# Retention and two expert layers on one core: q, k and v laid out by pairs of heads, states without zero blocks

## The chip, the cores and the metric

The kernel runs on one core of one Trainium2 chip. The metric is the time of one execution on the device, in microseconds (us). All data are float32. The engines are TensorE (PE in the rows; PEld are its weight loads), VectorE (DVE), ScalarE (ACT), GpSimd (POOL) and SyncE (SP), which here only issues copies.

## The reference, cut to what matters

```python
def _attn_ref(q, k, v):                      # each 4 x 8 x 576 x 64
    scale = 1.0 / np.sqrt(D_)
    scores = scale * np.matmul(q, k.transpose(0, 1, 3, 2))
    gamma = 1.0 - 2.0 ** (-5.0 - np.arange(H, dtype=np.float32))
    rel = pos[:, None] - pos[None, :]
    Dmat = np.where(rel >= 0, gamma[:, None, None] ** rel[None, :, :], 0.0)
    return np.matmul(scores * Dmat[None, :, :, :], v).astype(np.float32)
...
def reference(**kwargs):
    attn_out = _attn_ref(**attn_kwargs)
    x = np.ascontiguousarray(attn_out.transpose(0, 2, 1, 3)).reshape(B * S, H * D)
    x = _moe_ref(x=x, **moe_kwargs)
    return _moe2_ref(x=x, **moe2_kwargs)
```

The first step is a causal attention without softmax, whose weights decay by a power of `gamma` of the head. Its 2304 rows of 512 go through two expert layers (8 experts, 512 to 1024 to 512; one expert per row). The change is in the first step alone.

## The kernel before, in words

**Units.** `attention` (line 118) works in 20 units, five per batch. A main unit is a pair of heads over the first 512 positions, in four chunks of 128; four of them cover the eight heads. The fifth, the tail unit (`tail(u)`), has the last 64 positions of all eight heads. `gamma ** (i - j)` is split: q is multiplied by a power of its position (`qp`), v by the inverse power of its own (`vh`). Then a chunk needs no decay inside, and all chunks before it are summed in one state of 64x64 a head, the sum of k-transposed times vh.

**The steps of a unit.**
- `load` (133): SP copies q, k and v from their natural layout, k and v of each head apart: five copies of a main unit, six of a tail. A head's row of 64 values is a piece of 256 bytes (q: four rows, 1 KB).
- `prep` (170): `qp` and `vh`, on GpSimd from unit 2 on.
- `transposes` (191): TensorE turns k (part 0) and `qp` (part 1) chunk by chunk into PSUM, against the identity; ScalarE copies them to `kT` and `qT`.
- `scores` (207): eight matmuls, for each chunk and head kT by qT over 64 rows, the two heads in two row halves of the array and in two PSUM banks; VectorE multiplies with the mask `tri` into `P`.
- `state` (221): eight matmuls of 64 columns, k by vh, the two heads in two column halves; VectorE adds them up chunk by chunk and head by head into a 128x128 tile with a head's 64x64 state in each diagonal block. The other two blocks are zero from a memset at the start (lines 1513 to 1514).
- `inter` (240): the state before a chunk times that chunk's qT, three matmuls with 128x128 weights into the bank `O`; for a tail unit four, with the states after 512 positions, `st4`.
- `pv` (254): eight matmuls, vh by P, onto the same bank `O`, the heads in two column halves; ScalarE copies `O` to `xT`, the transposed output.

**Order.** `round_(u)` (284) interleaves the units: it prepares and transposes unit u+1, does `inter` of u-1, `scores` of u, `pv` of u-1 and `state` of u+1, and issues the copies of u+5. `slot()` puts a piece of background work between the steps: for a finished batch the router's logits (`logits4`, `token_logits`), the router itself (`Router.add`) and `row`, which transposes a tile of 128 rows back (`xps`) so that GpSimd can write it to its expert's list (`put`, line 486). When the rows of the first two batches are written, `gather` copies the rows of the first expert (`xb`), and the expert weights follow on SP. In `manual_schedule` the engines named in it (TensorE and GpSimd from round 1 on) run in the order of the code; a scheduler orders the others. The MoE behind it starts with `h` of its first place (line 851).

**PSUM.** Eight banks: two for transposes, two for scores, one for `state`, one for `O`, two for the background.

Of the kernel before, what the change touches and what calls it, by code (L numbers as in the profile page):

```python
# [53 lines left out]
TAB0, TAB1 = 72, 336  # L54
# [6 lines left out]
def host_tables():  # L61
# [3 lines left out]
    qtab = np.zeros((128, 4, 4, 2))  # L65
    for h in range(H):
        for t in range(5):
            vtab[:, h // 2, t, h % 2] = gam[h] ** (-(128.0 * t + p))
        for r in range(4):
            qtab[:, h // 2, r, h % 2] = gam[h] ** (4.0 * p + r) / 8.0  # L70
    tl = lambda sg: np.stack([[[gam[4 * j + 2 * a + h] ** (sg * (512.0 + t)) for h in range(2)] for a in range(2)] for j in range(2) for t in range(64)])
# [3 lines left out]
        "qtab": qtab.reshape(128, 32),  # L75
        "tri": p[:, None] <= p[None, :],
        "tri2": (p[:, None] <= p[None, :]) & (p[:, None] // 64 == p[None, :] // 64),
        "vtl": tl(-1).reshape(128, 4),
        "qtl": tl(1).reshape(128, 4) / 8.0,
# [17 lines left out]
    return {"tab": np.ascontiguousarray(tab)}, off  # L97
# [20 lines left out]
def attention(g, hooks):  # L118
# [6 lines left out]
    q, k, v = g.ia["q"], g.ia["k"], g.ia["v"]  # L125
# [7 lines left out]
    def load(u):  # L133
        s = st[u] = K()
        b, p = s.b, s.p = u // 5, u % 5
        if tail(u):
            s.raw = g.ld.tile([128, 3, 2, 2, DH], F32, tag="t", name=f"t{b}", bufs=2)
            for i, x in enumerate((k, q, v)):
                for j in range(2):
                    nc.sync.dma_start(out=s.raw[64 * j:64 * j + 64, i].rearrange("p a h d -> p (a h) d"),  # L140
                                      in_=x[b, 4 * j:4 * j + 4, 512:576].rearrange("h p d -> p h d"))
            return
        hs = slice(2 * p, 2 * p + 2)
        s.q = g.ld.tile([128, 2, 4, DH], F32, tag="q", name=f"q{u}")
        s.k = g.ld.tile([128, 4, 2, DH], F32, tag="k", name=f"k{u}")
        s.v = g.ld.tile([128, 4, 2, DH], F32, tag="v", name=f"v{u}")
        dq = lambda: nc.sync.dma_start(out=s.q, in_=q[b, hs, 0:512].rearrange("h (p r) d -> p h r d", r=4))

        def pair(x, d):
            for hh in range(2):  # L150
                nc.sync.dma_start(out=d[:, :, hh], in_=x[b, 2 * p + hh, 0:512].rearrange("(t p) d -> p t d", p=128))  # L151

        part = lambda c0, c1: nc.sync.dma_start(out=g.tab[:, c0:c1], in_=g.ia["tab"][:, c0:c1])
        if u:
            dq()
            pair(k, s.k)
        else:
            pair(k, s.k)
            part(0, TAB0)
            dq()  # L160
        pair(v, s.v)
        if u == 0:
            part(TAB0, TAB1)
        elif u == 3:
            part(TAB1, g.tab.shape[1])
            g.small_loads()
        elif u == 10:
            g.clear(1)

    def prep(u):  # L170

        s = st[u]
        s.vh = g.wk.tile([128, 4, 2, DH], F32, tag="vh", name=f"vh{u}", bufs=3)
        if tail(u):
            bc = [128, 2, 2, DH]
            s.qp = g.wk.tile([128, 4, 2, DH], F32, tag="qp", name=f"qp{u}")
            nc.gpsimd.tensor_mul(s.qp[:, 0:2], s.raw[:, 1], g.qtl[:, :, :, None].to_broadcast(bc))
            nc.gpsimd.tensor_mul(s.vh[:, 0:2], s.raw[:, 2], g.vtl[:, :, :, None].to_broadcast(bc))
            return
        s.qp = g.wk.tile([128, 4, 2, DH], F32, tag="qp", name=f"qp{u}")  # L180
        (nc.vector if u <= 1 else nc.gpsimd).tensor_mul(s.qp, s.q.rearrange("p h r d -> p r h d"),
                                                        g.qtab[:, s.p, :, :, None].to_broadcast([128, 4, 2, DH]))
        (nc.gpsimd if u else nc.vector).tensor_mul(s.vh, s.v, g.vtab[:, s.p, 0:4, :, None].to_broadcast([128, 4, 2, DH]))  # L183

    def flat(x):
        return x.rearrange("p h d -> p (h d)")
# [3 lines left out]

    def transposes(u, part):
        s = st[u]
# [1369 lines left out]
```

## Time and profile before

| | |
|---|---|
| median of three runs (lowest, highest) | 530.03 us (528.41, 531.34) |
| the profiled execution, its span | 528.95 us, 527.2 us |
| TensorE busy in the span | 507.8 us |
| VectorE, ScalarE, GpSimd busy | 300.3, 226.7, 142.4 us |
| `scores` of unit 0, of unit 4, of unit 19 start | 8.28, 29.32, 101.52 us |
| first expert matmul starts | 105.86 us |

The span goes from the first to the last instruction. A row of the timeline merges like instructions that follow each other; it gives start and length, the engine, the line of the kernel and what the instruction writes and reads, and in brackets the idle time before it with what ended it. TensorE runs one float32 matmul as two instructions (a transpose as one), so a count x8 in its timeline is four matmuls of the code. Ends of matmuls are modelled, so the cost of a step is best read from its start to the start of the next one.

### The profile page before, as it was taken

What the parts mean: (1) busy time and instruction counts of PE and PEld (TensorE: products, weight loads), DVE (VectorE), ACT (ScalarE), POOL (GpSimd) and SP (SyncE); (2) the same over time, 40 slices, a digit from 0 to 9 for tenths busy, and PEclk for the clock granted to TensorE, in tenths of its full rate; (3) what the DMA queues carried; (4) which work ended last, traced back from release to release, by engine and by line L of the source; (5) the groups of instructions that cost most, each with busy time, mean ns of one, the idle gap of its engine ahead of it and who ended that gap; (6) DMA issues with size and microseconds to landing.
All of it is one profiled execution on the core that took longest, in us unless ns stands there. A gap on an engine that the chain in (4) does not pass through costs nothing.

```text
span 527.2 us, 12238 instructions
## 1 busy us (share of the span) xinstructions
PE 507.8 (96%) x4427; PEld 478.0 (91%) x4427; DVE 300.3 (57%) x914; ACT 226.7 (43%) x440; POOL 142.4 (27%) x216
## 2 busy tenths in 40 slices
PE   7989999999999999999999999999999999999993
PEld 6779898799999999999999999999899889999992
DVE  6756668644537675857585866553656765522012
ACT  2344454333445554846464746432444434321120
POOL 3443748441204030230305070604210311110111
PEclk9999999999999999999999999999999999999997
DMA  8789996864989548475766755506769999988800
GB/s 198 165 206 196 255 218 167 268 252 152 291 224 286 164 150 222 142 207 187 203 203 191 212 176 179 158 16 187 244 199 326 320 282 256 312 280 281 278 35 33
DMA packets 133483, 109.64 MB, mean 208 GB/s; under 512 B 57477, under 2 KB 111109, under 8 KB 133413
## 3 DMA queue, kind: packets, MB, share of 16 engines
q1 hardware_dynamic: 127077, 94.69, 64.3%
q0 software_dynamic: 6336, 14.07, 7.2%
q8 instruction: 37, 0.61, 0.5%
q14 instruction: 33, 0.27, 0.2%
HBM read 93.44 MB, written 20.17 MB: 216 GB/s over the span
## 4 chain that ended last, share of the span: by engine, by line
PE 86%; DVE 4%; SPq 3%; DMA 3%; issue 1%; ACT 1%; POOL 1%; DVEq 0%; POOLq 0%; ACTq 0%
PE h L851 13%; PE y L927 9%; PE h L863 7%; PE h L862 7%; PE h L861 7%; PE y L931 6%; PE y L932 6%; PE y L930 6%; PE S L216 3%; PE yr L972 3%; PE O L258 3%; PE y L924 2%; SPq L151 2%; PE xps L656 2%; PE O L252 2%
## 5 line engine op out<-in xcount | busy, mean ns | idle before, releaser
L779 DVE TENSOR_TENSOR lo<-r,hi 128x1024 fp32r<-128x1024 f32 x80 | 97.7, 1223 | 49.7 <-ACT hi L779 47.7
L779 ACT CAST hi<-r 128x1024 fp32r<-128x1024 f32 x80 | 83.6, 1048 | 34.6 <-PE y L931 21.1
L931 PE MATMUL y<-hl,hi 128*128 128x316 f32 (+7 forms) x256 | 76.2, 299 | 0.3 <-DVE hl L867 0.3
L932 PE MATMUL y<-hh,lo 128*128 128x316 f32 (+7 forms) x256 | 76.0, 298 | 0.0
L930 PE MATMUL y<-hh,hi 128*128 128x316 f32 (+7 forms) x256 | 74.9, 298 | 0.0
L486 POOL DMA_INDIRECT xs<-x2s,idx x20 | 23.3, 1165 | 161.5 <-DVE hl L867 46.5
L927 PE MATMUL y<-hh,r 128*128 128x176 f32 (+3 forms) x384 | 60.3, 300 | 0.0
L866 ACT ACTIVATE hh<-h 128x316 fp32r<-128x316 f32 (+8 forms) x72 | 29.2, 406 | 70.6 <-PE h L863 70.5
L927 PEld LDWEIGHTS y<-hh,r 128*128 128x128 f32 x384 | 55.0, 190 | 0.0
L867 DVE SCALAR_TENSOR_TENSOR hl<-h,hh 128x316 fp32r<-128x316 f32 (+8 forms) x72 | 32.3, 448 | 38.2 <-ACT hh L866 38.1
L931 PEld LDWEIGHTS y<-hl,hi 128*128 128x128 f32 x256 | 48.2, 188 | 0.7 <-DVE hl L867 0.7
L932 PEld LDWEIGHTS y<-hh,lo 128*128 128x128 f32 x256 | 48.3, 188 | 0.0
L930 PEld LDWEIGHTS y<-hh,hi 128*128 128x128 f32 x256 | 47.7, 188 | 0.2
L858 ACT ACTIVATE hh<-h 128x176 f32<-128x176 f32 (+3 forms) x48 | 14.6, 305 | 75.6 <-PE h L851 74.9
L1131 POOL DMA_INDIRECT out<-o,oi x13 | 16.7, 1284 | 103.3 <-DVE o L1206 71.2
L949 DVE COPY yt<-y 128x176 f32<-128x176 f32 (+11 forms) x28 | 10.5, 390 | 44.0 <-ACT yt L951 40.6
L219 DVE TENSOR_TENSOR P<-S,tab 128x512 f32<-128x512 f32 (+1 forms) x40 | 23.6, 632 | 16.0 <-PE S L216 15.8
L183 POOL TENSOR_TENSOR vh<-v,tab 128x512 f32<-128x512 f32 x15 | 15.7, 1046 | 29.4 <-PE O L258 13.6
L1131 POOL DMA_INDIRECT out<-x2r,si x20 | 21.3, 1064 | 6.1 <-issue 5.2
L851 PE MATMUL h<-x_0h,r 128*128 128x160 f32 (+1 forms) x128 | 22.7, 311 | 0.0
L236 DVE TENSOR_TENSOR st<-st,kv 64x64 f32<-64x64 f32 x96 | 20.9, 218 | 3.0
L269 ACT COPY xT<-O 128x512 f32<-128x512 f32 x16 | 9.4, 585 | 30.6 <-PE O L258 30.6
(626 smaller groups left out, 1248.8 us busy)
## 6 DMA issues: line engine op xcount, KB each, us to landing
r<-w1a SPq DMA_DIRECT2D x32, 512.0 KB, 4.8
r<-w2a SPq DMA_DIRECT2D x32, 512.0 KB, 5.8
r<-w1b SPq DMA_DIRECT2D x32, 512.0 KB, 4.1
r<-w2b SPq DMA_DIRECT2D x32, 512.0 KB, 6.4
k<-k SPq DMA_DIRECT2D x32, 128.0 KB, 4.0
q<-q SPq DMA_DIRECT2D x16, 256.0 KB, 3.2
v<-v SPq DMA_DIRECT2D x32, 128.0 KB, 4.0
xb<-xs SPq DMA_DIRECT2D x12, 160.0 KB, 7.3
```

Source lines behind the costliest of these rows:

```text
L779: high, low = lambda: nc.scalar.copy(hi, raw), lambda: nc.vector.tensor_sub(lo, raw, hi.bitcast(F32))
L851: nc.tensor.matmul(ps, w.r1[:, c, fc], s.xh[:, c, 0:C], start=(c == 0), stop=(c == 3))
L861: nc.tensor.matmul(ps, w.hi1[:, c, fc], s.xh[:, c, 0:C], start=(c == 0), stop=False)
L862: nc.tensor.matmul(ps, w.hi1[:, c, fc], s.xl[:, c, 0:C], start=False, stop=False)
L863: nc.tensor.matmul(ps, w.lo1[:, c, fc], s.xh[:, c, 0:C], start=False, stop=(c == 3))
L866: nc.scalar.activation(s.hh[f], ps, AF.Relu)
L867: nc.vector.scalar_tensor_tensor(out=s.hl[f], in0=ps, scalar=0.0, in1=s.hh[f].bitcast(F32), op0=ALU.max, op1=ALU.subtract)
L927: nc.tensor.matmul(y, w.r2[:, f % 2, dc], s.hh[f], start=a, stop=o)
L930: nc.tensor.matmul(y, wh, s.hh[f], start=a, stop=False)
L931: nc.tensor.matmul(y, wh, s.hl[f], start=False, stop=False)
L932: nc.tensor.matmul(y, wl, s.hh[f], start=False, stop=o)
L1131: r = g.nc.gpsimd.indirect_dma_start(out=g.oa["out"][:, :].rearrange("n (b d) -> (n b) d", b=parts), out_offset=IndirectOffsetOnAxis(ap=id ...
```

## The change

The host program lays q, k and v out anew: for each main unit one block of 128 rows of 2048 values, k transposed, q transposed, k and v as before (`lay_out`), and for each tail unit one of 128 x 768. So `load` is one copy a unit, of 8 KB (tail: 3 KB) a partition; the first unit's comes in two halves. `transposes` is gone with its two banks and its copies. q is now scaled in its transposed layout, by a table `qt` of powers by position, one row of 128 copied and four chunks of powers made from it (`powers`, ScalarE). A state is a tile of 64 columns with the two heads under each other, and `inter` takes a matmul for each head. `scores` has three banks, `O` two.

```diff
+def lay_out(q, k, v):
+
+    q, k, v = (np.asarray(x, dtype=np.float32) for x in (q, k, v))
+    turn = lambda x: x[:, :, 0:512].reshape(B, 4, 2, 512, DH).transpose(0, 1, 2, 4, 3).reshape(16, 128, 512)
+    keep = lambda x: x[:, :, 0:512].reshape(B, 4, 2, 4, 128, DH).transpose(0, 1, 4, 3, 2, 5).reshape(16, 128, 512)
...
+    return {"main": np.ascontiguousarray(np.concatenate([turn(k), turn(q), keep(k), keep(v)], axis=2)),
+            "rest": np.ascontiguousarray(np.concatenate([rest(k, t), rest(q, t), rest(v, n)], axis=2))}
...
         if tail(u):
...
+            x = g.ld.tile([128, 768], F32, tag="t", name=f"t{b}", bufs=2)
+            nc.sync.dma_start(out=x, in_=g.ia["rest"][b])
+            s.kT, s.q, s.v = x[:, 0:256], x[:, 256:512], x[:, 512:768].rearrange("p (c h d) -> p c h d", c=2, h=2)
             return
...
+        x, src = g.ld.tile([128, 2048], F32, tag="m", name=f"m{u}"), g.ia["main"][4 * b + p]
+        s.kT, s.q = x[:, 0:512], x[:, 512:1024]
+        s.k, s.v = (x[:, o:o + 512].rearrange("p (c h d) -> p c h d", c=4, h=2) for o in (1024, 1536))
...
+        if u == 0:
+            nc.sync.dma_start(out=x[:, 0:1024], in_=src[:, 0:1024])
+            nc.sync.dma_start(out=g.qt[:, :, 0:128], in_=g.ia["qrow"])
+            part(0, TAB0)
+            nc.sync.dma_start(out=x[:, 1024:], in_=src[:, 1024:])
+            part(TAB0, TAB1)
         else:
...
+            nc.sync.dma_start(out=x, in_=src)
...
+    def prep_q(u):
...
+        elif u > 1:
+            nc.gpsimd.tensor_mul(s.qT, s.q, g.qt[:, s.p, 0:512])
+        else:
+            nc.vector.tensor_mul(s.qT[:, 0:128], s.q[:, 0:128], g.qt[:, s.p, 0:128])
+            for c in range(1, 4):
...
+    def powers(p):
+
+        for c in range(1, 5):
+            w = 128 if c < 4 else 64
+            nc.scalar.activation(g.qt[:, p, 128 * c:128 * c + w], g.qt[:, p, 0:w], AF.Copy, scale=g.qg[:, p, c - 1:c])
...
-        for hh in range(2):
-            h = slice(64 * hh, 64 * hh + 64)
-            for c in range(4):
-                x = kv[h, DH * c:DH * c + DH]
-                if c:
-                    nc.vector.tensor_add(s.st[c][h, h], s.st[c - 1][h, h], x)
-                else:
-                    nc.vector.tensor_copy(s.st[c][h, h], x)
+        for c in range(4):
+            x = kv[:, DH * c:DH * c + DH]
+            if c:
+                nc.vector.tensor_add(s.st[c], s.st[c - 1], x)
+            else:
+                nc.scalar.copy(s.st[c], x)
...
+        def mm(w, x, first):
+            for hh in range(2):
+                h = slice(64 * hh, 64 * hh + 64)
+                nc.tensor.matmul(s.O[h, w], x[h], s.qT[h, w], start=first, stop=False, skip_group_check=True)
...
         for c in range(1, 4):
-            cs = slice(128 * c, 128 * c + 128)
-            nc.tensor.matmul(s.O[:, cs], s.st[c - 1], s.qT[:, cs], start=c == 1, stop=False, skip_group_check=True)
+            mm(slice(128 * c, 128 * c + 128), s.st[c - 1], c == 1)
...
         if u and u + 1 < NU:
-            prep(u + 1)
+            prep_q(u + 1)
+            prep_v(u + 1)
         if u:
             slot()
-        if u + 1 < NU:
-            transposes(u + 1, 0)
-            if u:
-                slot()
-            else:
-                inter(0)
-                pv(0)
-            transposes(u + 1, 1)
-        if u > 1:
+        if u == 0:
+            inter(0)
+            pv(0)
+        elif u > 1:
             inter(u - 1)
...
             pv(u - 1)
+        if u:
+            slot()
         if u + 1 < NU and not tail(u + 1):
             state(u + 1)
...
-            g.ld = ac.enter_context(tc.tile_pool(name="ld", bufs=4))
+            g.ld = ac.enter_context(tc.tile_pool(name="ld", bufs=5))
...
-            g.psT = ac.enter_context(tc.tile_pool(name="psT", bufs=1, space=PSUM))
-            g.psS = ac.enter_context(tc.tile_pool(name="psS", bufs=2, space=PSUM))
-            g.psO = ac.enter_context(tc.tile_pool(name="psO", bufs=1, space=PSUM))
+            g.psS = ac.enter_context(tc.tile_pool(name="psS", bufs=3, space=PSUM))
+            g.psK = ac.enter_context(tc.tile_pool(name="psK", bufs=1, space=PSUM))
+            g.psO = ac.enter_context(tc.tile_pool(name="psO", bufs=2, space=PSUM))
```

How this moves instructions is seen at three places. First TensorE in round 13, before and after. In the names a digit behind the letters is the unit (Tk, Tq: the transposes; kv: `state`; O: `inter` and `pv`; S13_0: `scores` of head 0), r1R the router's ranks and xps a row tile.

```order
L258 MATMUL O11_1204<-P11_1113,vh11_961 64x128 x8
L228 MATMUL kv13_1236<-vh13_1161,k13_884 64x64 x8
L466 MATMUL r1R_1265<-oh1_79,utr_77 128x40
L467 MATMUL r1R_1265<-r1cum_1085,onesr_76 128x40
L199 MATMUL Tk14_1273<-ident_67,t2_948 128x128 x2
L656 MATMUL xps7_1278<-ident_67,xT1_732 128x128 x4
L199 MATMUL Tq14_1284<-ident_67,qp14_1262 128x128 x2
L252 MATMUL O12_1289<-qT12_1101,st3_0_143 128x128 x3
L656 MATMUL xps8_1293<-ident_67,xT1_732 128x128 x4
L216 MATMUL S13_0_1300<-qT13_1202,kT13_1176 128x128
```

```order
L263 MATMUL O11_905<-P11_851,vh11_738 64x128 x8
L663 MATMUL xps6_953<-ident_67,xT1_565 128x128 x4
L231 MATMUL kv13_959<-vh13_897,m13_684 64x64 x8
L473 MATMUL r1R_978<-oh1_76,utr_74 128x40
L474 MATMUL r1R_978<-r1cum_840,onesr_73 128x40
L249 MATMUL O12_986<-qT12_790,st3_0_141 64x128 x6
L663 MATMUL xps7_993<-ident_67,xT1_565 128x128 x4
L219 MATMUL S13_0_1000<-qT13_895,m13_684 128x128
```

The transposes of unit 14 are gone, `inter` has six matmuls in place of three, and a slot has moved behind `pv`.

Then VectorE around the masks of units 17 and 18, before and after; the transposition (L814, then L821) is that of the first expert's rows `xb1_0`.

```order
L219 TENSOR_TENSOR P17_1657<-S17_1_1659,tab_64 128x512
L238 COPY st3_1_144<-kv18_1679 64x64
L236 TENSOR_TENSOR st3_1_144<-st3_1_144,kv18_1679 64x64 x2
L236 TENSOR_TENSOR st4_1_146<-st3_1_144,kv18_1679 64x64
L238 COPY st3_1_144<-kv18_1679 64x64
L236 TENSOR_TENSOR st3_1_144<-st3_1_144,kv18_1679 64x64 x2
L236 TENSOR_TENSOR st4_1_146<-st3_1_144,kv18_1679 64x64
L814 STREAM_TRANSPOSE x1_0h_1833<-xb1_0_1602 128x5x2x32
L219 TENSOR_TENSOR P18_1718<-S18_0_1719,tab_64 128x512
```

```order
L222 TENSOR_TENSOR P17_1297<-S17_1_1299,tab_64 128x512
L821 STREAM_TRANSPOSE x1_0h_1475<-xb1_0_1253 128x5x2x32 x2
L237 TENSOR_TENSOR st3_1_142<-st3_1_142,kv18_1319 128x64 x2
L237 TENSOR_TENSOR st4_1_144<-st3_1_142,kv18_1319 128x64
L222 TENSOR_TENSOR P18_1347<-S18_0_1348,tab_64 128x512
```

Both transpositions have moved ahead of the sums of unit 18, which are three in place of eight.

Last the copies at the start on SP, before and after; k0, q0, v0 and m0 are those of unit 0.

```order
L151 DMA k0_152<-k 128x4x64 x2
L153 DMA tab_64<-tab 128x72
L147 DMA q0_151<-q 128x2x256
L151 DMA v0_153<-v 128x4x64 x2
L153 DMA tab_64<-tab 128x264
L147 DMA q1_161<-q 128x2x256
L151 DMA k1_162<-k 128x4x64 x2
L151 DMA v1_163<-v 128x4x64 x2
```

```order
L164 DMA m0_145<-main 128x1024
L165 DMA qt_139<-qrow 128x4x128
L162 DMA tab_64<-tab 128x56
L167 DMA m0_145<-main 128x1024
L162 DMA tab_64<-tab 128x260
L170 DMA m1_151<-main 128x2048
```

k and q of a unit come in one copy, and unit 1 is one copy in place of five.

## Rows read from the trace of the kernel before

**Rows 1.** The page: busy time of the engines; granted clock in 40 slices.
```profile
PE 507.8 (96%) x4427; PEld 478.0 (91%) x4427; DVE 300.3 (57%) x914; ACT 226.7 (43%) x440; POOL 142.4 (27%) x216
...
PEclk9999999999999999999999999999999999999997
```

**Rows 2.** Timeline of TensorE: scores of units 4 and 19, last inter, first expert matmul.
```profile
29.32 0.72 PE L216 MATMUL S<-qT,kT 64*128 64x128 f32 x8
...
101.52 0.71 PE L216 MATMUL S<-qT,kT 64*128 64x128 f32 x8
...
104.92 1.10 PE L248 MATMUL O<-qT,st 128*128 128x64 f32 x8
105.86 0.49 PE L851 MATMUL h<-x_0h,r 128*128 128x160 f32 x2
```

**Rows 3.** Stretches: length, busy us of each engine, clock, share and GB/s of DMA.
```profile
0.00:80.00 80.00, 73.00 (x929) 63.98 (x931) 51.78 (x193) 32.15 (x61) 37.16 (x55) 1.00 0.87 207
4.00:16.00 12.00, 9.40 (x106) 7.65 (x107) 7.01 (x19) 3.59 (x7) 4.08 (x4) 1.00 1.04 250
29.32:105.86 76.54, 75.18 (x966) 64.68 (x965) 53.41 (x209) 33.27 (x66) 41.83 (x58) 1.00 0.85 219
2.00:4.00 2.00, 2.00 (x12) 2.00 (x11) 1.24 (x1) 0.03 (x1) 1.21 (x3) 1.00 0.83 162
104.00:106.00 2.00, 2.00 (x14) 1.16 (x12) 0.00 (x0) 0.58 (x1) 0.00 (x0) 1.00 1.07 421
```

**Rows 4.** What TensorE waited for, 0 to 135 us: total, times, longest.
```profile
PE Tk L199 <- DMA k<-k: 1.8, 2, 1.5
...
PE O L252 <- ACT xT L269: 0.7, 1, 0.7
PE Tq L199 <- POOL qp L181: 0.5, 1, 0.5
```

**Rows 5.** Timeline of TensorE in rounds 13 and 14, without background work.
```profile
74.02 1.16 PE L216 MATMUL S<-qT,kT 64*128 64x128 f32 x16
75.11 1.09 PE L258 MATMUL O<-P,vh 128*64 128x128 f32 x16
76.14 0.66 PE L199 MATMUL Tk<-ident,k 128*128 128x128 f32 x4
76.63 0.60 PE L199 MATMUL Tq<-ident,qp 128*128 128x128 f32 x4
77.06 0.83 PE L252 MATMUL O<-qT,st 128*128 128x128 f32 x6
77.83 0.71 PE L216 MATMUL S<-qT,kT 64*128 64x128 f32 x8
78.47 1.09 PE L258 MATMUL O<-P,vh 128*64 128x128 f32 x16
79.40 0.63 PE L228 MATMUL kv<-vh,k 128*64 128x64 f32 x16
79.96 1.34 PE L339 MATMUL L<-xT,wg 128*32 128x512 f32 x8
```

**Rows 6.** Groups by line, 0 to 112 us: busy us, mean ns of one, idle before.
```profile
L236 DVE TENSOR_TENSOR st<-st,kv 64x64 f32<-64x64 f32 x96 | 20.9, 218 | 3.0
L219 DVE TENSOR_TENSOR P<-S,tab 128x512 f32<-128x512 f32 x32 | 20.6, 685 | 7.4 <-PE S L216 7.2
...
L183 POOL TENSOR_TENSOR vh<-v,tab 128x512 f32<-128x512 f32 x15 | 15.7, 1046 | 29.4 <-PE O L258 13.6 <-DMA v<-v 9.2 <-DMA t<-k 4.2
```

**Rows 7.** Timelines of GpSimd, SP and VectorE: row writes, the gather, its use.
```profile
58.80 0.97 POOL L486 DMA_INDIRECT xs<-xr,idx  x1 [0.30 <-issue]
...
87.69 1.03 POOL L486 DMA_INDIRECT xs<-xr,idx  x1 [0.16 <-issue]
...
90.51 1.91 SPq L712 DMA_DIRECT2D xb<-xs  x4
...
98.64 0.51 DVE L814 STREAM_TRANSPOSE x_0h<-xb 128x320 f32<-128x320 f32 x1
```

More of the change, by code (lines that the diff above doesn't have):

```diff
@@ L53 @@
 GATE, TOK, VAL = 512, 513, 514
-TAB0, TAB1 = 72, 336
+TAB0, TAB1 = 56, 316
 F32_MAX = 192
@@ L68, in host_tables @@
             vtab[:, h // 2, t, h % 2] = gam[h] ** (-(128.0 * t + p))
-        for r in range(4):
-            qtab[:, h // 2, r, h % 2] = gam[h] ** (4.0 * p + r) / 8.0
-    tl = lambda sg: np.stack([[[gam[4 * j + 2 * a + h] ** (sg * (512.0 + t)) for h in range(2)] for a in range(2)] for j in range(2) for t in range(64)])
+    own = lambda j: np.repeat(gam[2 * j:2 * j + 2], 64)[:, None]
+    qrow = np.stack([own(j) ** np.arange(128.0) / 8.0 for j in range(4)], axis=1)
+    qg = np.stack([own(j) ** (128.0 * np.arange(1, 5)) for j in range(4)], axis=1)
+    vtl = np.stack([[[gam[4 * j + 2 * a + h] ** (-(512.0 + t)) for h in range(2)] for a in range(2)] for j in range(2) for t in range(64)])
     one = np.ones((128, 1))
@@ L188, in chunks @@
+    def powers(p):
+        for c in range(1, 5):
+            w = 128 if c < 4 else 64
+            nc.scalar.activation(g.qt[:, p, 128 * c:128 * c + w], g.qt[:, p, 0:w], AF.Copy, scale=g.qg[:, p, c - 1:c])
     def chunks(u):
         return range(2 if tail(u) else 4)
-    def transposes(u, part):
-        s = st[u]
-        w = 256 if tail(u) else 512
-        nm = "k" if part == 0 else "q"
-        ps = g.psT.tile([128, 512], F32, tag="T" + nm, name=f"T{nm}{u}")
-        for c in chunks(u):
-            cols = slice(c, 512, 4) if part and not tail(u) else slice(128 * c, 128 * c + 128)
-            x = s.qp[:, c] if part else s.raw[:, 0, c] if tail(u) else s.k[:, c]
-            nc.tensor.transpose(ps[:, cols], flat(x), g.ident)
-        xT = g.wk.tile([128, 512], F32, tag=nm + "T", name=f"{nm}T{u}", bufs=3 if part else 2)
-        nc.scalar.copy(xT[:, 0:w], ps[:, 0:w])
-        if part:
-            s.qT = xT
-        else:
-            s.kT = xT
@@ L246, in inter @@
                 o = 128 * (p % 2) + 64 * (p // 2)
-                w = slice(o, o + 64)
-                nc.tensor.matmul(s.O[:, w], g.st4[s.b % 2][:, p], s.qT[:, w], start=p == 0, stop=False, skip_group_check=True)
+                mm(slice(o, o + 64), g.st4[s.b % 2][:, p], p == 0)
             return
         for c in range(1, 4):
-            cs = slice(128 * c, 128 * c + 128)
-            nc.tensor.matmul(s.O[:, cs], s.st[c - 1], s.qT[:, cs], start=c == 1, stop=False, skip_group_check=True)
+            mm(slice(128 * c, 128 * c + 128), s.st[c - 1], c == 1)
     def pv(u):
@@ L316, in attention @@
     with g.tc.manual_schedule(engines={T.PE, T.DVE, T.Activation}):
-        prep(0)
-        transposes(0, 0)
-        transposes(0, 1)
+        prep_q(0)
+        prep_v(0)
+        scores(0)
         state(0)
-        scores(0)
-        prep(1)
+        prep_q(1)
+        prep_v(1)
+        powers(2)
+        powers(3)
         round_(0)
+        powers(0)
+        powers(1)
     with g.tc.manual_schedule(engines={T.PE, T.Pool}):
@@ L1509, in build @@
             g.first = first
[L1511 to L1514 removed]
+            g.st3 = [ap.tile([128, 3, DH], F32, name=f"st3_{i}") for i in range(2)]
+            g.st4 = [ap.tile([128, 4, DH], F32, name=f"st4_{i}") for i in range(2)]
             main3, tail3, g.step3 = tokens_out(g, 3)
```

93 lines of the change are left out of this document (34 added, 59 removed).

## The prediction

> **What bounds the kernel now.** I read the page first: TensorE is busy for 507.8 of 527.2 us and its granted clock is full up to the last slice [rows 1]. So the question is what the change takes out of TensorE's row, and in which stretch. Then the timeline of TensorE: the first expert matmul of the MoE, at 105.86 us [rows 2], marks the end of what the change touches; behind it the same instructions run in the same loops. Ahead of it there are two regimes, and the table of stretches parts them. From the scores of unit 4 (29.32 us, [rows 2]) to 105.86 us TensorE is busy for 75.18 of 76.54 us [rows 3]: there a microsecond less of TensorE is a microsecond less of the kernel. Ahead of 29.32 us it waits again and again for the copies of q, k, v and for the scaling behind them (the largest group is the first of [rows 4]). In the first 80 us the DMA engines are busy for 87% and yet move only 207 GB/s; from 104 to 106 us, when expert weights are what SP has in flight, 421 GB/s at the same full share [rows 3]. What attention loads is expensive by its pieces, not by its size.
>
> **Part 1, the transposes.** A main unit loses eight transposes. Four of k cost 0.49 us (76.14 to 76.63), four of q 0.43 us (76.63 to 77.06) [rows 5]; together 0.92 us. A tail unit loses four, half of that, 0.46 us. In all 16 x 0.92 + 4 x 0.46 = 16.6 us of TensorE's time. The transposes of units 0 to 5 lie ahead of the scores of unit 4, in the first regime, and are counted there (part 4). In the second regime are units 6 to 19, eleven main and three tail: 11 x 0.92 + 3 x 0.46 = 11.5 us, all on the path. The copies of kT and qT out of PSUM went on ScalarE beside TensorE's work; that they go gives nothing by itself.
>
> **Part 2, states without zero blocks.** In a main unit `inter` had three matmuls with 128x128 weights and 128 columns; now it has six with 64x64 weights, in pairs on opposite corners of the array. No row of before shows that form. Old cost: 77.06 to 77.83, 0.77 us, or 0.26 us each [rows 5]. The nearest rows are the two kinds of pairs that share the array: eight matmuls of `pv` (128x64 weights, 128 columns) take 0.93 us (78.47 to 79.40), 0.116 us each, and eight of `scores` (64x128 weights) 1.09 us (74.02 to 75.11), 0.136 us each. Six at these prices are 0.70 to 0.82 us, so the change is between -0.07 and +0.05 us and I take 0. The bound on the other side is that the corners do not run together (first rival). In a tail unit four matmuls of 64 columns took 0.94 us (104.92 to 105.86, [rows 2]); they become eight of 64 columns, and the nearest row is `state`, eight of 64 columns in 0.56 us (79.40 to 79.96). Gain 0.38 us a tail, 1.5 us in all; at worst none.
> What the rows show is overlap where the two matmuls of a pair lie in different row halves and different PSUM banks (`scores`), and where they lie in different column halves of one bank (`pv`). The new pair has different row halves and one bank. I lean to the rows, since the two corners also write different partitions, as in `pv`. The Trainium skill, page "TensorEngine Tiling (Array Packing)", section "Gotcha 1: PSUM Pressure", says: "Different row tiles cannot access same PSUM bank simultaneously". By that rule the corners would follow one another, and the sum would be that of the first rival; no row of this trace has two row halves in one bank, so the trace neither agrees nor differs.
> On VectorE eight state sums of 0.22 us [rows 6] become three, and one copy on ScalarE: 1.1 us a unit, off the path. It makes cover: VectorE keeps 2 x 0.69 + 3 x 0.22 = 2.0 us per main unit [rows 6], beside some 4 us of TensorE and the router's small operations.
>
> **Part 3, waits in the second regime.** Two waits of [rows 4] go: 0.5 us for the scaled q (nothing needs it before the next round now) and 0.7 us for the copy that freed the only O buffer (now there are two). New ones can come at two places. GpSimd keeps two multiplications of 1.05 us a unit [rows 6]; a round with two row writes asks it for 2 x 1.05 + 2 x 1.27 (0.97 and a gap of 0.30, [rows 7]) = 4.6 us, against rounds of about 4. And on VectorE both transposes of the first expert's rows now stand ahead of the state sums and masks of unit 18, so these wait there for the gather. Before, VectorE came to them at 98.64 us, 11 us after the last row write at 87.69, and did not wait; the gather was issued from 90.51 to 92.42 [rows 7]. Now the sums of unit 18 (1.8 us) and two rounds of transposes (1.8 us) are no longer between, so it comes there about 7.4 us after that write, while the gathered rows lie in SBUF between 5 us (end of the issue) and 11 us after it: 0 to 3.6 us of waiting on VectorE, of which TensorE sees only what goes beyond the two or so it has before it needs the masks of unit 18. I take 1 us for all new waits, near the lower end since both queues have slack, range 0 to 3.
> Sum of the second regime: 11.5 + 1.5 + 1.2 - 1.0 = 13.2 us.
>
> **Part 4, the start.** Here the copies set the pace. In the queue up to the block of unit 2 stand 0.52 (k and q of unit 0) + 0.26 + 0.03 (tables) + 0.52 (the rest of unit 0) + 0.13 + 2 x 1.05 = 3.6 MB, up to that of unit 3 4.6 MB. From 2 to 4 us the queues move 162 GB/s, later 250 GB/s [rows 3], so moving starts in effect at 2 + 2 x (1 - 162/250) = 2.7 us. The rate of runs of 4 to 8 KB is not in this trace. Its bounds are 250 GB/s, which the short pieces reach from 4 to 16 us with the engines full, and 421 GB/s for the weights [rows 3]; I take 390, near the weights, the longest runs there are. Unit 2 then lies in SBUF at 2.7 + 9.2 = 11.9 us. GpSimd makes its qT and vh, 2 x 1.05, and `state` of unit 2 starts at 14.0. From there TensorE sets the pace: state 0.56, inter 0.77, scores 1.09, pv 0.93, the same four for the next unit, and inter 0.77 [rows 5] are 7.5 us, and the scores of unit 4 start at 21.5 us. (Unit 3 arrives at 14.5 and is scaled by 16.6; wanted at 17.4.) Before they started at 29.32: gain 7.8 us, of which some 5 are the transposes of units 0 to 5. At 421 GB/s it is 8.5. At 250 GB/s unit 3 arrives at 21.1, its vh is ready at 23.2, and state, inter, scores, pv and inter (4.1 us) put the scores of unit 4 at 27.3: gain 2.0.
> The small operations that build qT of units 0 and 1 and the table of powers (8 on VectorE in place of two multiplications, 16 on ScalarE) are costed at nothing: ScalarE waits for TensorE there, and VectorE does them while the rest of unit 0 and unit 1 are still on the way. Without that cover they are 4 x 0.2 us or so, at the size of the state sums. SP issues one copy a unit in place of five, so it cannot be later than before.
>
> **Sum.** 13.2 + 7.8 = 21.0 us. The profiled execution took 528.95 us (span 527.2 and 1.75 around it): 528.95 - 21.0 = 507.95. It lies 1.08 us under the median of 530.03, so for the median I forecast 509.0 us.
>
> **Rivals.**
> First, the corners follow one another. Six matmuls then cost up to 6 x 0.26 = 1.54 us in place of 0.77: 16 x 0.77 = 12.3 us, of which about 2 hide at the start, and the 1.5 us of the tails do not come: 509.0 + 11.8 = 520.8 us. For it: no row shows such a pair in one bank. Against it: `pv` shares a bank and overlaps.
> Second, slower than before: the loads become the bound. The change copies more, 16 x 1.05 + 4 x 0.39 = 18.4 MB where q, k and v are 14.2 MB, since k comes in both layouts; with tables, cleared rows and nine row writes some 22 MB pass before the last unit. If the long runs were no faster than the mean of the first 80 us, 207 GB/s [rows 3], the last block would land at 2.7 + 106 = 109 us and, scaled, let the scores of unit 19 start at 111 us instead of 101.52 [rows 2]: 539 us. It decides at 22 MB in 97 us, 227 GB/s; at 250 GB/s there is still a gain of some 8 us. For it: engines that are 87% busy now. Against it: 421 GB/s at the same busy share.
> Third, the waits of part 3 at their upper end: 511 us, a variant of the forecast.
> That the change does not do what it says is ruled out: in its order of instructions no transpose of k or q stands on TensorE.
>
> **Chances.** Forecast 0.77 (its own range 505 to 516, from 421 GB/s and no new wait to 250 GB/s); waits at the upper end 0.05; corners in sequence 0.12; loads as the bound, at least as slow as before, 0.04; a mix that leaves less than half a per cent, 0.02. The range 504 to 516 us takes in the first two. A difference of about 0.5% (2.7 us) is what a measurement of this kernel can tell from none. Faster by more 0.94, within it 0.02, slower by more 0.04.
>
> **What would show it.** Right: scores of unit 4 near 21.5 us, first expert matmul near 85 us, no idle TensorE of more than 1 us between; six `inter` matmuls in 0.7 to 0.8 us; over 300 GB/s in the first 15 us. Wrong: `inter` at 1.3 us or more (first rival); `state` late unit after unit, with DMA behind GpSimd (second); VectorE waiting for the gather and `pv` of unit 18 for its mask (third). If the first expert matmul comes 21 us earlier and the end does not, then what follows was held by something other than TensorE, such as its weight copies, and the argument itself would be wrong.

## The result, and the profile after

The changed kernel takes 521.63 us (median of six runs, 520.81 to 523.61) against 530.27 us for the kernel before, taken beside it: ratio 0.9859, 95% interval 0.9837 to 0.9881. It is faster, by 8.6 us. The forecast was 509.0 us with a range of 504 to 516: too fast by 12.6 us, and the range is missed. The profiled execution took 523.61 us, two above the median.

The rows that answer [rows 2], from the timeline of TensorE (start, us, engine, line, operation): scores of unit 4, one inter of a main unit, one of a tail, the first expert matmul.
```profile
24.18 0.71 PE L219 MATMUL S<-qT,t 64*128 64x128 f32 x8
...
40.79 0.87 PE L249 MATMUL O<-qT,st 64*64 64x128 f32 x12
41.60 1.16 PE L219 MATMUL S<-qT,m 64*128 64x128 f32 x16
...
46.65 0.68 PE L249 MATMUL O<-qT,st 64*64 64x64 f32 x16
47.26 1.16 PE L219 MATMUL S<-qT,m 64*128 64x128 f32 x16
...
98.38 0.54 PE L858 MATMUL h<-x_0h,r 128*128 128x160 f32 x2
```
Scores of unit 4 start at 24.18 us (forecast 21.5, before 29.32). The first expert matmul starts at 98.38 (forecast near 85, before 105.86). So the start gave 5.1 us, and the second regime is 74.20 us long where it was 76.54: 2.3 us of the 13.2 that the sum promised. Six inter matmuls take 0.81 us (40.79 to 41.60), those of a tail 0.61 (46.65 to 47.26), or 0.75 in front of a group of transposes (27.58 to 28.33).

The stretches that answer [rows 3] (length, busy us of PE, PEld, DVE, ACT and POOL, granted clock, share and GB/s of DMA):
```profile
4.00:14.00 10.00, 7.81 (x70) 6.71 (x71) 5.53 (x14) 2.44 (x9) 1.08 (x1) 1.00 1.00 392
24.18:98.38 74.20, 67.95 (x971) 53.19 (x969) 45.03 (x149) 21.18 (x49) 45.62 (x59) 0.98 0.75 246
98.38:521.70 423.32, 410.37 (x3207) 0.99 0.69 206
```
The copies run at 392 GB/s, as forecast. In the second regime TensorE's busy time fell from 75.18 to 67.95 us, but it now stands still for 6.25 us of it, where before it was 1.36. What it waits for, 0 to 130 us (answers [rows 4]: total, times, longest):
```profile
PE pf L502 <- DVE st L237: 2.8, 1, 2.8
PE kv L231 <- POOL vh L183: 1.6, 2, 1.0
...
PE kv L231 <- DVE st L237: 1.5, 1, 1.5
...
PE S L219 <- DVE P L222: 0.8, 1, 0.8
```
Behind the largest is one row of VectorE. The timelines of VectorE, GpSimd, ScalarE and TensorE, and two stretches with the granted clock behind it (length, busy us of TensorE, clock, share and GB/s of DMA):
```profile
54.00 3.39 DVE L382 TENSOR_TENSOR r1sh<-L,r1mx 128x40 f32<-128x40 f32 x1
...
60.57 0.17 DVE L463 TENSOR_TENSOR C<-r1cum,oh 128x8 fp32r<-128x8 f32 x1
...
53.88 1.04 POOL L183 TENSOR_TENSOR vh<-m,tab 128x512 f32<-128x512 f32 x1
54.87 0.18 POOL L644 COPY xr<-tab 128x5 f32<-128x5 f32 x1
54.99 0.11 POOL L645 MEMSET xr<- 128x25 f32 x1
55.06 1.26 POOL L193 TENSOR_TENSOR qT<-m,qt 128x512 f32<-128x512 f32 x1
56.29 1.04 POOL L183 TENSOR_TENSOR vh<-m,tab 128x512 f32<-128x512 f32 x1
...
57.42 0.24 ACT L383 ACTIVATE r1sh<-r1sh 128x40 f32<-128x40 f32 x1 [5.05 <-DVE r1sh L382]
...
60.88 0.24 PE L502 MATMUL pf<-C,onesr 128*128 128x8 f32 x1 [2.79 <-DVE st L237]
61.05 1.16 PE L219 MATMUL S<-qT,m 64*128 64x128 f32 x16
62.15 1.98 PE L263 MATMUL O<-P,vh 128*64 128x128 f32 x16
64.05 1.12 PE L663 MATMUL xps<-ident,xT 128*128 128x128 f32 x4
...
62.00:63.00 1.00, 1.00 (x12) 0.57 0.00 0
63.00:64.00 1.00, 1.00 (x12) 0.50 0.74 123
```
A subtraction of 128x40 that takes 0.19 us elsewhere (with q on VectorE, below) lasts 3.39 us, until 57.39, when the row of multiplications on GpSimd ends (57.33). All that stands behind it in VectorE's queue is late with it, down to the counts `C`, done at 60.74. TensorE's `pf` reads `C` and starts 0.14 us later, after a wait of 2.79 us. (The view puts this wait down to the state sums, which `pf` does not read; in every kernel below in which `pf` waits, it starts 0.14 or 0.15 us after `C`. ScalarE's exponential is late as well, and the copies behind it, but the copy that VectorE's sums need is done at 58.72, long before.) Then TensorE's granted clock falls from 1.00 to 0.50, from 2.4 to 1.2 GHz, and `pv` takes 1.90 us (62.15 to 64.05), not 1.03 as in front of the other rows' transposes.

### The profile page after: what moved, and what is told of

Same layout as the page of the kernel before. It is cut to its first block, busy times and chain, and to the rows that moved or that the text cites. A ratio compares the mean times of both kernels' runs of the same rounds, so it can differ in the third digit from the quotient of the medians.

```text
span 521.7 us, 11984 instructions
## 1 busy us (share of the span) xinstructions
PE 498.2 (95%) x4411; PEld 464.2 (89%) x4411; DVE 288.0 (55%) x840; ACT 213.8 (41%) x432; POOL 142.8 (27%) x210
## 4 chain that ended last, share of the span: by engine, by line
PE 74%; DMA 10%; DVE 7%; issue 3%; SPq 2%; ACT 2%; POOL 1%; POOLq 0%; DVEq 0%; ACTq 0%
PE h L858 13%; PE y L934 9%; PE h L869 5%; PE h L870 5%; PE h L868 5%; PE y L938 5%; PE y L939 5%; PE y L937 5%; PE O L263 3%; PE S L219 3%; DMA rows<-xs 2%; PE y L931 2%; DMA xb<-xs 2%; PE yr L979 2%; PE O L249 2%
## 5 line engine op out<-in xcount | busy, mean ns | idle before, releaser
L222 DVE TENSOR_TENSOR P<-S,tab 128x512 f32<-128x512 f32 (+1 forms) x40 | 23.8, 632 | 13.5 <-PE S L219 13.4
L219 PE MATMUL S<-qT,m 64*128 64x128 f32 x256 | 20.0, 295 | 2.4 <-DVE qT L195 1.6
L263 PE MATMUL O<-P,vh 128*64 128x128 f32 x288 | 21.9, 296 | 0.0
```

Of the source, the lines that this page charges most:

```text
L219: nc.tensor.matmul(S[hh][:, c], s.kT[hp, cs], s.qT[hp, cs], start=True, stop=True)
L263: nc.tensor.matmul(s.O[64 * hh:64 * hh + 64, 128 * c:128 * c + 128], s.vh[:, c, hh], s.P[:, hh, c], start=False, stop=True, skip_group_che ...
```

## Experiments

Theory H: GpSimd's multiplications in a row hold VectorE's small operations, and that is where the waits and the fall of the clock come from. Theory F: a change between array tiles of different shape costs TensorE time, and the transposes of rows (`xps`), which shared their shape with those of q and k, now pay it alone. Theory W: TensorE at half its rate at the start delays unit 4. Each kernel below is timed against the kernel before on its own chip (527.9 to 528.8 us there), so the ratios compare better than the times.

**One multiplication less on GpSimd.** First q's, then instead v's, moved to VectorE:
```diff
-            nc.gpsimd.tensor_mul(s.qT, s.q, g.qt[:, s.p, 0:512])
+            nc.vector.tensor_mul(s.qT, s.q, g.qt[:, s.p, 0:512])
```


> The changed kernel, with the scaling of q for units 2 and later (pairs of heads; tails stay) on VectorE instead of GpSimd. Theory H (held operations): VectorE's small router operations with two SBUF inputs stand still while GpSimd multiplies without a gap, so r1sh<-L,r1mx took 3.39 us and r2s 3.00 us; TensorE then waited 2.8 us at 60.88, and its granted clock fell to 0.50. With one multiplication of 1.05 us per round left on GpSimd no such operation should take over 1.2 us, the wait of 2.8 should be under 0.5, no clock under 0.95 between 20 and 95 us, and the time 521.6 - 2.5 - 1.7 - 1 to 2 = 515 to 517. Rival Q (it is GpSimd's queue that runs late, because of the puts, and the held operations cost nothing): only the waits of kv for vh (together 3 us in the second regime) go, the wait for the router stays, and the time is 519 to 521. Rival V (VectorE becomes the bound: 14 multiplications of about 0.7 us more on it): S waits for qT in the rounds with router work, 521 to 525.

> The changed kernel with the scaling of v (not of q) on VectorE for all pairs of heads; GpSimd keeps that of q, 1.27 us per unit, and that of the tails. Theory H (two multiplications in a row on GpSimd hold VectorE's small operations): it does not matter which of the two goes; nothing on the router's lines over 1.4 us, pf waits under 0.6 us, and the time is 514 to 517, as with q on VectorE (514.6). Rival (what mattered was q's dependence, scaled late on GpSimd): S waits for qT from GpSimd in rounds with the puts, and the time is 518 to 522.

Measured: 514.64 us, ratio 0.9748 (0.9731 to 0.9765), and 515.17 us, 0.9751 (0.9713 to 0.979). It does not matter which of the two goes. With q on VectorE, in the stretch from the scores of unit 4 to the first expert matmul:
```profile
21.75:88.94 67.19, 65.87 (x970) 51.70 (x968) 45.55 (x161) 21.57 (x49) 32.72 (x47) 1.00 0.84 276
```
and on VectorE and GpSimd:
```profile
51.97 0.19 DVE L382 TENSOR_TENSOR r1sh<-L,r1mx 128x40 f32<-128x40 f32 x1
...
53.25 0.99 DVE L371 TENSOR_TENSOR oh<-tab,r1mn 128x40 fp32r<-128x40 f32 x1
...
53.13 1.05 POOL L183 TENSOR_TENSOR vh<-m,tab 128x512 f32<-128x512 f32 x1 [2.63 <-DVE P L222]
```
The same subtraction is back at 0.19 us; one operation of the router is still held, for 0.99 us, to the end of the single multiplication (54.18). The wait of pf is 0.3 us and the clock in this stretch is full. Q and V fall. The scaling on VectorE is itself held at times. One of q took 2.09 us (44.74), and the state sums behind it made TensorE wait 0.89 us, until 47.47; in the other kernel one of v took 2.21 us, and no wait of TensorE stands behind it.

**The factor at the end.** The factor of a query belongs to a column of O, so it can be applied as O leaves PSUM, and q needs no scaling. (The kernel also has a sixth buffer for blocks, and the tables of the first two pairs are made before round 0, those of the others behind it; before it was the other way round.)
```diff
-        s.qT = g.wk.tile([128, 512], F32, tag="qT", name=f"qT{u}", bufs=3)
...
+        s.qT = s.q
...
-            nc.scalar.copy(g.xT[b][:, s.p, 64 * odd:64 * odd + 512], s.O)
+            nc.vector.tensor_mul(g.xT[b][:, s.p, 64 * odd:64 * odd + 512], s.O, g.qt[:, s.p, 0:512])
```


> The changed kernel with q not scaled ahead at all: scores and the state products read q from its block, and the row factor is applied where the result leaves PSUM, by one VectorE multiplication of PSUM with the table in place of ScalarE's copy; a sixth buffer for blocks stands in place of the three of the scaled q. Theory H (VectorE held by two multiplications in a row on GpSimd): as with q on VectorE, 515 to 517, and since the first scores need no scaled q, they start when their block lands, near 5.3 us instead of 6.86, S of unit 4 near 23 instead of 24.18. Theory W (TensorE works at half its rate until about 14 us because it stood 1.6 us before the first scores): without that stop the first scores take 1.16 instead of 2.08 and the states' products, P products and kv of units 0 and 1 their later durations, 3 us more: together 511 to 514. Rival V (VectorE as bound): 519 to 524.

Measured: 513.37 us, 0.9724 (0.9707 to 0.974). From the scores of unit 4:
```profile
22.38:89.00 66.62, 66.17 (x971) 51.59 (x969) 45.45 (x162) 13.29 (x33) 29.48 (x44) 1.00 0.80 270
```
TensorE stands still for 0.45 us of 66.62. This is the second regime without new waits at full clock; it is 3.3 us longer than the 63.3 forecast. The time lies in the range that I had given to H and W together, but the gain that W promised is not in it: TensorE stood still here too (1.36 us for v of unit 0), its granted clock was 0.50 from 10.2 to 13.4, and unit 4 comes at 22.38, later than with q on VectorE. The low clock costs the start 0.6 us here: v of unit 2 is scaled by 14.03, and its state products, behind slow work, start at 14.66.

**A multiplication that nobody needs.** On the kernel with the factor at the end:
```diff
+            if u > 1:
+                x = g.wk.tile([128, 512], F32, tag="spare", name=f"spare{u}", bufs=1)
+                nc.gpsimd.tensor_mul(x, s.q, g.qt[:, s.p, 0:512])
```


> The kernel with the row factor applied at the end (513.4 us; GpSimd multiplies once per unit there), and a spare multiplication of q by its table on GpSimd behind that of v, whose result nobody reads. The work of GpSimd is that of the changed kernel again, but nothing waits for the spare result. Theory H (GpSimd's multiplications in a row hold VectorE's small operations with two inputs from SBUF): operations of 2.2 to 3.4 us come back on VectorE's router lines, TensorE's wait of pf for st is 2 us or more, with a lower granted clock behind it, and the time is 516.5 to 519.5. Rival D (the waits of the changed kernel came from the dependence on the scaled q, or from v scaled late behind it): nothing is held over 1.2 us, pf waits under 0.5, and the time is 513 to 514.

Measured: 522.55 us (520.78 to 524.58), 0.9875 (0.9844 to 0.9906): 9 us more than without it (8 by the ratios), above the range that I gave to H. (The profiled execution is the slowest of the four, with a granted clock of 0.95 in most stretches where the others have 1.00; the fastest is still 7.4 us above the median without the spare multiplication.) VectorE, GpSimd, TensorE:
```profile
53.05 4.55 DVE L375 TENSOR_TENSOR r1sh<-L,r1mx 128x40 f32<-128x40 f32 x1
...
56.28 1.25 POOL L186 TENSOR_TENSOR spare<-m,qt 128x512 f32<-128x512 f32 x1
...
61.02 0.35 PE L495 MATMUL pf<-C,onesr 128*128 128x8 f32 x1 [3.81 <-DVE st L229]
61.29 2.08 PE L211 MATMUL S<-m 64*128 64x128 f32 x16
```
The held operation is back, for 4.55 us, to 57.60, where the spare multiplication ends (57.53); so are the wait (3.81 us) and the fall of the clock. The stretch from the scores of unit 4 to the first expert matmul is 74.79 us (22.87 to 97.66), against 66.62. No result was waited for: D falls, and it is GpSimd's work itself that does it.

**TensorE kept busy to the first scores.**
```diff
-    for i in range(8):
+    for i in range(16):
         nc.tensor.matmul(ps[:, 0:128], g.zero, g.zero, start=True, stop=True)
```


> The changed kernel with 16 matmuls on zeroes before the first scores instead of 8, so that TensorE is busy from 1.48 us until the first scaled q is there at 6.8. Theory W (the stop of 1.6 us before the first scores is what leaves TensorE at half its rate until 14 us): the first scores take 1.1 to 1.3 us instead of 2.08, products of units 0 and 1 likewise, S of unit 4 starts 2 to 3 us earlier (21.2 to 22.2 instead of 24.18) and the time is 518.5 to 519.6. Rival L (the slow products have another cause, the arrival of the loads or the operands): S of unit 4 stays within 0.5 us of 24.2 and the time at 521 to 522.

Measured: 520.71 us, 0.9844 (0.9812 to 0.9876), as the changed kernel. In the changed kernel the first scores began at 6.86, after a stop of 1.61 us, and took 2.08. (The record gives a granted clock of 1.00 there all the same, 4 to 14 us; it is the duration that shows the lower rate.) Here TensorE shows:
```profile
7.55 1.16 PE L219 MATMUL S<-qT,m 64*128 64x128 f32 x16
...
15.41 0.69 PE L231 MATMUL kv<-vh,m 128*64 128x64 f32 x16 [1.80 <-POOL vh L183]
16.02 1.06 PE L249 MATMUL O<-qT,st 64*64 64x128 f32 x12
17.01 2.08 PE L219 MATMUL S<-qT,m 64*128 64x128 f32 x16
```
W is right that without the stop the first scores run at their later rate, and the gain is nothing: the state products of unit 2 then wait 1.80 us for v, scaled behind the arrival of block 2, and the clock falls behind that wait. In seven of the kernels unit 4 comes 7.7 us after the state products of unit 2: 16.46 and 24.18 in the changed kernel, 14.03 and 21.75 with q on VectorE, 14.66 and 22.38 with the factor at the end; here it is 9.3, with the low clock. Here and in the changed kernel the arrival of block 2 and the scaling behind it set the start, not TensorE's rate.

**Rows of tokens in pairs.** Eight transposes in one place of the order, nothing in the next:
```diff
+    both = lambda t: lambda: (rows[t](), rows[t + 1]())
...
-    return [logits, choose, rows[0], rows[1], None, rows[2], step, rows[3]] + [None] * (b // 2) + [puts]
+    return [logits, choose, both(0), None, None, None, step, both(2)] + [None] * (b // 2) + [puts]
```


> The changed kernel with the transposes of two rows of tokens (eight transposes of 128x128) in one place of the order instead of four in each of two places. Theory F (the array's change of shape costs, and a group of four transposes that stands alone pays it in full, while before it shared it with those of q and k): a pair takes 0.58 + 0.44 = 1.02 us in all instead of 2 x 0.58 = 1.16, and the matmuls behind the place that now has no transposes lose 0.03 to 0.07 each; the sum over 18 rows of tokens is at most 2 us, hardly seen in one time. Rival (no such cost): a pair takes 1.16 us and nothing else gets shorter.

Measured in one run: 518.24 us, not enough to tell from 521.63. Its timeline, and the one of the changed kernel, behind `pv` in the round of unit 5:
```profile
29.60 1.09 PE L663 MATMUL xps<-ident,xT 128*128 128x128 f32 x8
30.62 0.69 PE L231 MATMUL kv<-vh,m 128*64 128x64 f32 x16
31.24 0.87 PE L249 MATMUL O<-qT,st 64*64 64x128 f32 x12
...
33.13 1.09 PE L263 MATMUL O<-P,vh 128*64 128x128 f32 x16
34.06 0.64 PE L231 MATMUL kv<-vh,m 128*64 128x64 f32 x16
```
```profile
30.59 0.66 PE L663 MATMUL xps<-ident,xT 128*128 128x128 f32 x4
31.18 0.69 PE L231 MATMUL kv<-vh,m 128*64 128x64 f32 x16
31.80 0.66 PE L663 MATMUL xps<-ident,xT 128*128 128x128 f32 x4
32.38 0.87 PE L249 MATMUL O<-qT,st 64*64 64x128 f32 x12
...
34.27 1.09 PE L263 MATMUL O<-P,vh 128*64 128x128 f32 x16
35.30 0.66 PE L663 MATMUL xps<-ident,xT 128*128 128x128 f32 x4
```
From start to start a group alone costs 0.59 and 0.58, a pair 1.02; `pv` in front of a group costs 1.03 (and 1.02 in front of `inter`, 42.69 to 43.71), in front of state products, which share its tile shape, 0.93; state products behind a group cost 0.62, behind `pv` 0.56. From the scores of unit 5 to those of unit 7 it is 8.85 us with pairs (27.92 to 36.77) and 9.30 without (28.91 to 38.21): 0.22 us a pair, as F says. The Trainium skill, page "TensorEngine Tiling (Array Packing)", section "Key Properties", has it that a change of the tiling mode, as against one of tile, drains TensorE; it gives no price. These rows agree that a change of shape costs time, and by them it is 0.05 to 0.15 us at a neighbour.

**Zero blocks again,** on the kernel with the factor at the end: 128x128 states, one product for both heads (six state sums and two copies a unit).
```diff
-            for hh in range(2):
-                h = slice(64 * hh, 64 * hh + 64)
-                nc.tensor.matmul(s.O[h, w], x[h], s.qT[h, w], start=first, stop=False, skip_group_check=True)
+            nc.tensor.matmul(s.O[:, w], x, s.qT[:, w], start=first, stop=False, skip_group_check=True)
```


> The kernel with the row factor applied at the end (513.4 us), with the states of two heads as 128x128 blocks with zeroes again and one product for both heads. Theory F (a change between 128x128 tiles and 64-row or 64-column tiles costs TensorE about 0.1 to 0.15 us, and the step without zero blocks made every neighbour of the rows' transposes another shape): products of states take 0.67 to 0.77 instead of 0.80, the rows' transposes that stand next to them 0.44 to 0.54 instead of 0.58, tails 0.93 instead of 0.61 to 0.75; VectorE adds states in six operations instead of three. In sum 511.5 to 513.5: the step without zero blocks is worth nothing or less. Rival C (two corners really save time, as 2 x 0.30 against 3 x 0.23 would): the time is 514.5 to 517.

Measured: 521.94 us, 0.987 (0.9844 to 0.9895), 8.6 us more than with the factor at the end (7.7 by the ratios); my expectation was wrong. Its timeline of TensorE:
```profile
21.48 0.82 PE L220 MATMUL kv<-vh,m 128*64 128x64 f32 x16 [2.33 <-DVE st L228]
...
30.93 0.71 PE L208 MATMUL S<-t 64*128 64x128 f32 x8
...
39.30 0.83 PE L238 MATMUL O<-m,st 128*128 128x128 f32 x6
40.06 1.16 PE L208 MATMUL S<-m 64*128 64x128 f32 x16
```
F's prices hold where they were meant: products of states 0.76 beside a group of transposes, and that group 0.50 (38.80 to 39.30) where it was 0.59. But the start is lost: unit 4 at 30.93, 8.55 us later. Of this 6.8 us lie ahead of the state products of unit 2 (21.48 against 14.66): copies and sums of states now follow each other in a chain, `inter` of unit 0 waits 1.08 us for a copy, these products 2.33 us for six sums among masks, and the clock is low in between. In this kernel, and in the next, ScalarE loads its table of functions in the middle of that chain (1.28 us at 9.99; in the other kernels at 0.75), so its start overstates what the zero blocks cost; how much is not settled. In the second regime the step without zero blocks is worth 1.7 us (68.33, to the first expert matmul at 99.26, against 66.62).

**Zero blocks and pairs.** The kernel of the last step with the rows in pairs as well.

> The kernel with the row factor applied at the end (513.4 us), with states as 128x128 blocks and with two rows of tokens transposed in one place. Theory F: a pair next to a product of states shares its shape, 0.44 + 0.44 to 0.54, and the time is 1 to 2.5 us below that with full states alone. Rival: pairs save nothing there, and the time is that of full states within 0.5 us.

Measured: 523.18 us, 0.9903 (0.988 to 0.9926): no gain by pairs here. The second regime is 68.90 us, against 68.33. TensorE waits 3.4 us in all for state sums in this kernel, 2.3 in the one above; F's gain of 1 to 2.5 us did not show, and cannot be told from these waits.

**A better start.** Factor at the end, pairs, and matmuls on zeroes between the first scores and the first state products (four, in a second kernel six); the row table behind block 0, and in the second kernel behind block 1.
```diff
         scores(0)
+        for i in range(4):
+            nc.tensor.matmul(ps[:, 0:128], g.zero, g.zero, start=True, stop=True)
         state(0)
```


> The kernel with the row factor applied at the end (513.4 us), with two more edits: at the start the column table and the second half of block 0 are loaded ahead of the row table, and four matmuls on zeroes stand between the first scores and the first state products; and two rows of tokens are transposed in one place instead of two. Theory W (after a stop of over a microsecond TensorE runs at half its clock for some 3 us, as the granted clock of 0.50 from 10.4 to 13.3 us shows): without the stop of 1.36 us at 7.07 no clock of 0.5 before 20 us, S of unit 4 near 20.5 instead of 22.38. Theory F (pairs save 0.22 us each, 8 pairs): another 1.5 to 2. In sum 509 to 511. If neither holds: 513 to 514.

> The row factor applied at the end, rows of tokens transposed in pairs, six matmuls on zeroes between the first scores and the first state products, and the row table (256 KB) loaded behind the block of unit 1 instead of ahead of it. In the kernel of the third step the state products of unit 1 waited 1.11 us at 12.77 because block 1 landed late. If that wait is the load's place in the queue, 256 KB at 400 GB/s give back 0.6 us of it: S of unit 4 near 22.3 instead of 22.90, no granted clock under 0.95 before 90 us, time 511 to 512 and ratio to the kernel before 0.966 to 0.969. Rival: ScalarE's multiplications for the table now stand in the way of the copies of unit 1's first state, and S of unit 4 is at 23 or later.

Measured: 512.14 us, 0.9687 (0.9668 to 0.9707), the lowest time of all, and 512.99 us (511.69 to 515.5), 0.971 (0.9682 to 0.9737). In the first, no clock below full up to 90 us, although stops of 1.29 and 1.11 us stayed, but unit 4 at 22.90 (not 20.5): the state products of units 1 and 2 waited 1.11 and 0.63 us for v, scaled behind the arrival of their blocks. In the second, scores of unit 1 waited 1.45 us for their block, the clock was 0.50 from 14 to 16 us, and unit 4 came at 24.98: on the rival's side, but not for the rival's reason. Block 1 came no earlier for its new place in the queue (GpSimd takes it up at 11.65, in the first at 11.67). So the start is set by when blocks land, and in the second by the clock behind that wait too. Pairs gave 1.2 us: the second regime is 65.40 us in both, against 66.62. Six of the eight pairs lie there, 0.20 us each, as F says.

## Why the prediction was wrong

What was right: the start came from the copies at 392 GB/s (forecast 390), and the corners overlap. Six inter matmuls take 0.80 to 0.81 us, at the upper end of 0.70 to 0.82; in sequence they would take 1.54. So the **first rival** is false, although its 520.8 us is nearly the time measured: a time that fits does not prove a mechanism. The rule of the Trainium skill weighed there (page "TensorEngine Tiling (Array Packing)", section "Gotcha 1: PSUM Pressure") differs from this trace for two row halves that write different partitions of one bank; the measurement decides. The **second rival** (loads) is not there: `state` waited for v twice, 0.64 and 0.97 us, and not unit after unit. Nor is the third's place (VectorE waiting for the gather): its transposes at 90.47 wait for nothing.

The span is 521.7 us, and 527.2 - 21.0 = 506.2 was forecast, so 15.5 us are to be found. (From median to median the miss is 12.6: the execution profiled before lies 1.1 us under the median that the forecast started from, the one after 2.0 above its own.)

- **Part 3 is the step that failed: waits, 5.1 us, and the clock behind them, 1.8.** I took 1.0 us for new waits, range 0 to 3, and 1.16 us of idle time in all; it is 6.25. Of this, 5.1 us stand behind held operations of VectorE: 2.79 behind the subtraction, 0.81 behind `r2s` (3.00 us at 77.77) and 1.54 behind `r2cum` and `C` (1.77 at 82.06, 0.97 at 83.87). I costed GpSimd's queue as a queue only: is the product there in time? "Both queues have slack" was about that, and it was nearly so (1.0 us for a late vh). What I left out is that VectorE stands still beside it. Two rows of the kernel before said so (below), and I had not read them as that: VectorE's L364 took 1.64 us and L455 0.95, both ending with a multiplication on GpSimd. I also priced both multiplications at 1.05 us, while that of q now reads a full table in place of one value per head: 1.27. The clock's price is the difference in TensorE's busy time, 67.95 against 66.17 with the factor at the end. That a wait costs again by the clock behind it stood nowhere in my sum.

```profile
84.03 1.64 DVE L364 TENSOR_TENSOR oh<-tab,r2mn 128x32 fp32r<-128x32 f32 x1
...
86.24 0.95 DVE L455 TENSOR_TENSOR r2cum<-r2cum,oh 128x8 fp32r<-128x8 f32 x1
...
84.53 1.07 POOL L181 TENSOR_TENSOR qp<-q,tab 128x512 f32<-128x512 f32 x1
86.12 1.04 POOL L183 TENSOR_TENSOR vh<-v,tab 128x512 f32<-128x512 f32 x1 [0.52 <-PE O L258]
```

- **Parts 1 and 2, transposes and tails, 4.0 us too much.** Busy time in the second regime was to be 75.18 - 11.5 - 1.5 = 62.2 us; without waits and with full clock it is 66.17. I priced the transposes by the rows of before (0.43 to 0.49 each group), as if what remains cost the same without them. But with them went the neighbours of the same shape: a row's transposes, 0.44 to 0.53 before, now cost 0.59, and 0.05 to 0.13 more at the steps beside (`inter` in front of a row took 0.67 before and takes 0.80 now). By the comparison of pairs a place is worth 0.22 us; 13 rows stand there alone, some 3 us. And I priced all four tails by the dearest, 0.94: they took 0.83, 0.93, 0.84 and 0.94 us, and take 0.75, 0.61, 0.75 and 0.61, which is 0.8 us in all and not 1.5. The rest is the choice of kernel to compare with: with the factor at the end the router's logits take 0.1 to 0.2 us longer each time. With v on VectorE, where TensorE stands still for only 0.13 us in this stretch, it is busy for 65.60; by that kernel the clock costs 2.4 us and parts 1 and 2 are 3.4 too much.
- **Part 4, the start, 2.7 us.** The mechanism was right and a size was off: state products of unit 2 began at 16.46 us, not 14.0. Block 2 had landed at 14.14, not 11.9. By then 236 GB/s x 2 us + 392 GB/s x 10 us = 4.4 MB had moved, where I had counted 3.6; I put that down to the blocks behind it, already in flight. In the eight kernels with other edits but the same copies up to this block it landed between 12.77 and 13.58, so about a microsecond of this term may be this execution's own. GpSimd then needed 2.3 us, not 2.1. From there 7.7 us to unit 4, as forecast (7.5).
- **Behind the first expert matmul, 2.0 us**, 423.3 against 421.3 before. Eight of the other kernels show 421.1 to 422.2 there, two 424.3 and 425.1, and the profiled execution of the changed kernel is 2 us above its median. I put it down to that execution; it was not tried.

Together 5.1 + 1.8 + 4.0 + 2.7 + 2.0 = 15.6.

Of the signs that were to show it, the two start times failed too (24.18 and 98.38 us), but "no idle TensorE of more than 1 us between" is the one that failed and named the place. The waits of part 3 were a rival as well (the third), but at 511 us and in another place.

## What to carry to other kernels

Taking work off the bounding engine brings the others closer together in time: read each small row of VectorE that is long for its size against GpSimd's timeline, and count multiplications on GpSimd as time in which VectorE's operations with two inputs in SBUF may stand still. Price what is removed by what its neighbours cost without it, above all where a step shares its tile shape with the next. A wait of 2 to 4 us on TensorE, as here, is to be charged with the slower clock behind it.

## What the runs showed of the hardware

In these traces VectorE's operations with two inputs in SBUF stand still while GpSimd multiplies, and not for one instruction alone: 3.39 us across three multiplications and 4.55 us across four, with the small copies between. The Trainium skill, page "SBUF — State Buffer", section "SBUF: two separate sides", says that such a VectorE operation and one of GpSimd that reads SBUF cannot run at once: whichever starts first locks a shared pair of ports for the whole instruction, and the other is blocked. The rows agree that VectorE stands still; that it can go without a turn over several instructions of GpSimd is more than the page says. Not all of it is multiplications: `r2s`, held for 3.00 us, began at 77.77, while GpSimd was still on a row write (77.45 to 78.43), and what held it until the first multiplication the rows do not show.

After a stop TensorE's granted clock can fall, from 2.4 to 1.2 GHz: in the changed kernel it stood still from 58.1 to 60.88 us, the clock was 1.00 until past 62 and 0.50 from then to past 65. With the spare multiplication it was 0.50 by 59, still within the stop (57.2 to 61.02). Not every stop does it: behind those of 0.97, 0.81 and 1.54 us in the same stretch of the changed kernel no fall is seen, behind one of 1.36 us at the start (factor at the end) there is one, and behind 1.29 and 1.11 us (better start) none. What decides is open.
